# FNet mixing and a gated FFN on one core: batch 1 joins the folded sequence transform, and its tables are made a batch earlier

## The chip, the cores and the metric

The kernel runs on one core of a Trainium2 chip. The metric is the device time in microseconds (us). The engines are TensorE (PE for its matmuls, PEld for its weight loads), VectorE (DVE), ScalarE (ACT), GpSimd (POOL) and SyncE (SP, which here issues nearly all DMA transfers). Matrix products accumulate in PSUM; everything else lies in SBUF or in device memory.

## What is computed

```python
batch, seq, dim = (8, 3008, 256)
n_tokens, d_model, d_ff = (24064, 256, 1536)
...
X = np.fft.fft(x, axis=1)
X = np.fft.fft(X, axis=2)
mixed = X.real.astype(np.float32).reshape(B * S, D)
...
gate = 1.0 / (1.0 + np.exp(-(mixed @ w_gate)))
val = mixed @ w_val
return (gate * val @ w_out).astype(np.float32)
```

All is float32. The real part of a two-dimensional Fourier transform over the sequence (3008) and the features (256), and on it a gated feed-forward layer with 1536 hidden features.

## The kernel before

**The feature transform is folded into the weights.** The weights are multiplied on chip by the feature cosines and sines, which gives G1 and G2 (tables of 256 x 1536 for gate and value). What is left for each batch is the sequence transform: a cosine part pk and a sine part qk, each 128 features x 1505 frequencies. By symmetry a frequency and its mirror image come out of the same two products: their sum and their difference.

**The main loop** (L1213) has 576 iterations i: 8 batches, 6 chunks of 252 frequencies (chunk 5 has 246), 12 tiles of 128 hidden features. 72 iterations are one batch (`per`), 12 one chunk (`i0`). In iteration i:

- PE does front_a(i), the four matmuls pf<-pk; back, ten products po of an iteration five earlier with the output weights; and front_b(i), the four matmuls pf<-qk, which end what front_a began.
- ACT does the sigmoid of iteration i-1 (L880, h<-pf), the copy ae (L866) of front_a's result, the seeds of iteration i+1's PSUM (L851, pf<-ek,ge) and the second sigmoid (L894, pf<-z).
- DVE does z (L881, ae less pf), the two products h (L893, L897), and between the two one operation more (`gap[i]` where there is one, else one of the output sums c<-c of `later`). After front_b come two or three more of `later`: the output of a finished chunk as sums, 32x32 transposes (L995, os<-c) and stores (L1011, L1015).
- POOL does the sums sf<-h (L903) by which the back products need fewer matmuls.

Each engine works through its own instructions in the order of the program. Everything else is hung into this loop by tables written out by hand: `at(i, f)` puts f at the end of iteration i (any engine), `gap[i]` puts a DVE operation between the two products, `mid[i]` puts PE work in the middle. Side work is: loads and folds of the next batch's x, its sequence transform, tables and output.

**The sequence transform exists in three forms.** Batch 0 has no fold beyond the one of the mirror images and is done before the loop, with the tables ST[0] (cosines and sines of 128 partitions x 6 x 753). Batch 1 has the "half" form: x is copied by DMA to device memory (xr) in mirrored order (mirror_x, L179) in two copies of 768 KB and six of 256 KB, loaded (load_x, L147), folded by POOL and DVE (feat, across, swap, turn), and at i=64 the function `whole` does 96 pairs of matmuls of 63 rows, ev and od, for both blocks and both parts at one place. Batches from 2 on have the "quarter" form: quarter_x (L150 on, 23 DMAs: 3 that write zeros, 18 of 128 KB, 2 of 384 KB), more folding on POOL and DVE, and `quarter(b, blk)` at two places of the loop, 96 matmuls of 32 rows and 95 columns each (sum<-st), whose results are spread by DVE (quarter_ends, 19 operations placed one in each iteration).

**The tables of the quarter form are made on chip, in batch 1.** The sines and cosines come from the same input table `stab`: table_rows (L274, six DMAs to rtab in device memory, rows reversed), then quarter_load (L308, 16 DMAs into the raw tables odd and ev) and quarter_small (24 small DMAs for the factors self, other and angle), then sums on POOL and DVE (`four`, `eight`), ACT copies (`ends`, `compact`, scaling by a half) and small DVE operations (`turns`, `ratios`, `cross`: tangents and ratios). They lie at i=65 to 99 (per+1 to per+27), in a tile `st` that takes the place of batch 1's tables.

**Batch 0's first chunk** (chunk 0, whole_) has no sf sums: its output weights are WO and its product is two 504-column matmuls (po<-h,wc) in each iteration. Its two output halves are stored in 32 DMAs.

**The DMA queue.** SP issues transfers in program order; stores, loads of x, copies to xr and rtab, table loads and the rows ek for the seeds (L839) stand in one line.

Two places that a sentence can't say well: which side work stands where (`mid` and `gap` are looked up in the loop as below), and the SP-ordered copies.

```python
between = gap.pop(i, [])
if not between and later and i < count - 8:
    between = [later.pop(0)]
    n -= 1
...
mid.get(i, lambda: None)()
...
for f in side.pop(i, []):
    f()
```

Of the kernel before, what the change touches and what calls it, by code (L numbers as in the profile page):

```python
# [53 lines left out]
NQ = 6  # L54
NP = 128
# [26 lines left out]
def kernel(  # L82
# [28 lines left out]
    NJ = NO // 2 + 1  # L111
# [67 lines left out]
    def mirror_x(b):  # L179

        if b > 1:
            return quarter_x(b)

        copy = nc.sync.dma_start
        src = xf[b]
        dst = XR[b] = dram.tile([P, 4, NQ, D], F32, name=f"xr{b}")
        ops = [lambda: copy(out=dst[HP - 2 : HP, :, NQ - 1],
                            in_=zero[:, :, 0:D].to_broadcast([2, 4, D]))]

        def rows(par):  # L190
            copy(out=dst[par * HP : (par + 1) * HP, :, 0:N3], in_=src[0:HP, :, par:NQ:2])

        def mirror(par, q):
            t = M // 2 - 2 * q - par
            lo, p0, n = par * HP, t // NQ, HP - 2 * ((par, q) == (0, N3 - 1))
            copy(out=dst[lo : lo + n, :, N3 + q].rearrange("p h d -> h p d"),
                 in_=src[p0 - n + 1 : p0 + 1, :, t % NQ].rearrange("p h d -> h p d")[:, ::-1])
        for par in range(2):
            ops.append(lambda par=par: rows(par))
            ops += [lambda par=par, q=q: mirror(par, q) for q in range(N3)]  # L200
        return ops


    dt = const.tile([P, 2, D], F32, name="dt")
    ST = [const.tile([P, 2, NQ, NE + NO], F32, name="st", tag="st")]
# [14 lines left out]
    def load_table(t, q, n, lo=0, hi=NE + NO):  # L220
        nc.sync.dma_start(out=ST[0][0:NP, t, q : q + n, lo:hi], in_=stab[:, t, q : q + n, lo:hi])

    def table_again():

        full = const.tile([P, 2 * NQ * (NE + NO)], F32, name="st", tag="st")
        sizes = (2 * N3 * (NE + NO), 2 * N3 * NJ, 2 * NO, N3, N3)
        at_ = [sum(sizes[0:i]) for i in range(6)]
        st, jt, eo, *tans = [full[:, at_[i] : at_[i + 1]] for i in range(5)]
        ST[:] = [st.rearrange("p (t q k) -> p t q k", t=2, q=N3),
                 jt.rearrange("p (t q k) -> p t q k", t=2, q=N3),  # L230
                 eo.rearrange("p (h k) -> p h k", h=2), *tans]
        for t in range(2):
            for par in range(2):
                nc.sync.dma_start(out=ST[0][par * HP : (par + 1) * HP, t], in_=stab[0:HP, t, par:NQ:2])

    def table_odd():

        odd, j4 = ST[0][:, :, :, NE:], ST[1]
        pool = nc.gpsimd

        def inner(t):
            pool.tensor_tensor(j4[:, t, :, 1 : NJ - 1], odd[:, t, :, 2::2], odd[:, t, :, 1 : NO - 1 : 2],
                               op=ALU.add)

        def half(t):
            nc.scalar.mul(j4[:, t, :, 1 : NJ - 1], j4[:, t, :, 1 : NJ - 1], 0.5)

        def ends():
            pool.tensor_copy(j4[:, 0, :, 0:1], odd[:, 0, :, 0:1])
            pool.memset(j4[:, 1, :, 0:1], 0.0)  # L250

            for par in range(2):
                rows = slice(par * HP, (par + 1) * HP)
                pool.tensor_copy(j4[rows, par, :, NJ - 1 :], odd[rows, par, :, NO - 1 :])
                pool.memset(j4[rows, 1 - par, :, NJ - 1 :], 0.0)

        def tangent():
            nc.vector.reciprocal(ST[4], odd[:, 0, :, 0])
            nc.vector.tensor_tensor(ST[3], odd[:, 1, :, 0], ST[4], op=ALU.mult)
            nc.vector.tensor_scalar(out=ST[4], in0=ST[3], scalar1=-1.0, scalar2=None, op0=ALU.mult)  # L260
        return tangent, lambda: inner(0), lambda: half(0), lambda: inner(1), lambda: half(1), ends


# [14 lines left out]
    def quarter_tables():  # L278

        full = const.tile([P, 2 * NQ * (NE + NO)], F32, name="st", tag="st")  # L280
        wide = 2 * NQ4
        sizes = dict(e4=2 * N3 * NQ4, j4=2 * N3 * NQ4, r4=2 * N3 * NQ4, eo=6 * NO, tan=N3, less=N3, angle=2 * N3,
                     self=2 * N3, other=2 * N3, cx=N3, cy=N3, sign=1, odd=2 * N3 * NO, ev=2 * N3 * NE)
        lo = 0
        for name, n in sizes.items():
            TAB[name] = full[:, lo : lo + n]
            lo += n
        assert lo <= full.shape[1]
        TAB["at"] = lo - sizes["odd"] - sizes["ev"]
        TAB["full"] = full  # L290
        TAB["sums"] = full[:, TAB["at"] : TAB["at"] + 16 * wide].rearrange("p (b w x h k) -> p b w x h k", b=2, w=2, x=2,
                                                                           h=2)
        for name in ("ev", "e4", "j4", "r4", "odd"):
            TAB[name] = TAB[name].rearrange("p (t q k) -> p t q k", t=2, q=N3)
        eo = TAB["eo"].rearrange("p (i k) -> p i k", i=6)
        TAB["eo"] = [[eo[:, 4 + w].rearrange("p (h k) -> p h k", h=2) for w in range(2)],
                     [eo[:, 2 * w : 2 * w + 2] for w in range(2)]]

# [12 lines left out]
    def quarter_small(i):  # L311
        for g, par, lo in TILES:
            if i == 2:
                for t in range(2):
                    nc.sync.dma_start(out=TAB["angle"][lo : lo + TB, t * N3 : (t + 1) * N3],
                                      in_=quarter_src(g, par, t, NE))
            else:
                for h, col in enumerate((0, NE)):
                    nc.sync.dma_start(out=TAB[("self", "other")[i]][lo : lo + TB, h * N3 : (h + 1) * N3],
                                      in_=quarter_src(g ^ i, par, 0, col))  # L320

    def quarter_ops():
# [6 lines left out]
        def clear():  # L329
            for x in (j4, r4, e4):  # L330
                pool.memset(x[:, :, :, 0 :: last], 0.0)
            for g, par, lo in TILES:
                pool.memset(sign[lo : lo + TB], (1.0, -1.0)[g])

        def turns():
            vec.reciprocal(TAB["less"], TAB["angle"][:, 0:N3])
            vec.tensor_tensor(TAB["tan"], TAB["angle"][:, N3:], TAB["less"], op=ALU.mult)
            vec.tensor_scalar(out=TAB["less"], in0=TAB["tan"], scalar1=-1.0, scalar2=None, op0=ALU.mult)

        def ratios():  # L340
            vec.reciprocal(TAB["self"], TAB["self"])
            vec.tensor_tensor(TAB["other"], TAB["other"], TAB["self"], op=ALU.mult)
            vec.tensor_scalar(out=TAB["other"], in0=TAB["other"], scalar1=sign, scalar2=None, op0=ALU.mult)

        def cross():

            vec.reciprocal(TAB["cy"], ev[:, 0, :, 1])
            vec.tensor_tensor(TAB["cx"], ev[:, 1, :, 1], TAB["cy"], op=ALU.mult)
            vec.tensor_scalar(out=TAB["cx"], in0=TAB["cx"], scalar1=sign, scalar2=None, op0=ALU.mult)
            vec.tensor_scalar(out=TAB["cy"], in0=TAB["cx"], scalar1=-1.0, scalar2=None, op0=ALU.mult)  # L350
# [24 lines left out]
        return clear, (turns, lambda: eight(0), lambda: eight(1), ratios, cross), (lambda: four(0), lambda: four(1)), (  # L375
# [167 lines left out]
    def fold_ops(b, nq):  # L543
# [25 lines left out]
        if b == 1:  # L569
# [5 lines left out]
            for q in qs:  # L575
                ops += [lambda blk=blk, q=q, e=pool if q is qs[-1] else nc.vector: across(e, blk, q) for blk in range(2)]
# [7 lines left out]
        if b:  # L584
# [8 lines left out]
            tan = lambda: (ST[3], ST[4]) if b == 1 else (TAB["tan"], TAB["less"])  # L593
# [22 lines left out]
            def turn(q, minus):  # L616

                y = [slots[:, q : q + 16 : 15], slots[:, q + N3 : q + N3 + 10 : 9]]
                if minus:
                    y.reverse()  # L620
                nc.vector.scalar_tensor_tensor(
                    out=y[0][:, :, HD:D], in0=y[1][:, :, 0:HD], scalar=tan()[minus][:, q : q + 1],
# [27 lines left out]
    def half(b, w, d, blk, sn, other=None):  # L650


        c0, n = ((0, NE), (NE, 2 * NJ if b else NO))[blk]
        ev, od = [bank(name, other and other[i])[:, 0:n] for i, name in enumerate(("ev", "od"))]

        def sums(*qs):
            for q in sorted(qs, key=lambda q: q % 2):
                mm((ev, od)[q % 2], w(q), ST[0][0:NP, int(sn), q, c0 : c0 + n], q < 2, q >= NQ - 2)

        def both():  # L660

            for r in range(2):
                for q in range(N3):
                    for par, sum_ in enumerate((ev, od)):
                        rows = slice(par * HP, par * HP + HP - 1 - (par and q == N3 - 1))
                        if blk:
                            out_, wq = sum_[:, r * NJ : (r + 1) * NJ], q + N3 * r
                            tab = ST[1][rows, r ^ int(sn), q]
                        else:
                            out_, wq = sum_[:, r::2], q + N3 * (r ^ int(sn))  # L670
                            tab = ST[0][rows, int(sn), q, r:NE:2]
# [634 lines left out]
```

## Time and profile before

| | |
|---|---|
| time, median of 3 runs | 1912.32 us (1912.19 to 1915.45) |
| the profiled execution | 1912.46 us, of which the span (first to last instruction) is 1910.7 us |
| TensorE clock granted | 1.00 |
| busy PE, DVE, ACT, POOL | 99%, 79%, 71%, 81% of the span |
| one iteration of the loop | 3.12 us (3.05 to 3.09 in chunk 5) |
| one batch, from i=144 to 216 | 230.5 us; batch 1, from 72 to 144, 233.3 us |
| DMA | 58 GB/s in the mean, 652 stores of 56 and 7 KB |

The profile gives busy times of each engine, the chain of waits that ended last, groups of instructions by source line, what each wait was for, and a timeline. An iteration of the loop is read from PE's timeline as the distance between two successive groups pf<-pk.

### The profile page before, as it was taken

Reading aid. Unit: us, or ns where it says so; the run is one execution under the profiler, and the core shown is the slowest. Engines: PE = TensorE matmul, PEld = TensorE weight load, DVE = VectorE, ACT = ScalarE, POOL = GpSimd, SP = SyncE. Lnnn points to the kernel's source line nnn. Section 1 sums busy time; section 2 is a strip of 40 time slices with the busy share of each in tenths; the row PEclk is TensorE's granted clock in tenths of the full one; section 3 lists DMA queues with packets and bytes.
Section 4 is the critical chain, followed back from the end, with each engine's and each line's share of the span. In section 5 each row is a group of like instructions: output and inputs, shape, how many; then the busy total and the mean of one; then the engine's idle time right before and its main releaser. Section 6 shows DMA issues by size and latency. Waiting matters only on the chain.

```text
span 1910.7 us, 35839 instructions
## 1 busy us (share of the span) xinstructions
PE 1899.5 (99%) x11740; PEld 1759.9 (92%) x11740; DVE 1513.2 (79%) x3351; ACT 1351.7 (71%) x3219; POOL 1543.8 (81%) x2742
## 2 busy tenths in 40 slices
PE   8999999999999999999999999999999999999999
PEld 5789999899999999999999999999999999999998
DVE  7677777878979778787788878888788787977775
ACT  4877767767777777767777777777767777777775
POOL 2489969987999779997799878999789986877770
PEclk9999999999999999999999999999999999999999
DMA  8353234312122121221211222112120220011011
GB/s 314 109 98 68 71 102 100 77 39 81 20 61 59 31 84 26 69 42 36 88 37 52 45 39 81 39 50 56 30 76 16 36 39 14 15 24 18 15 18 30
DMA packets 198833, 110.05 MB, mean 58 GB/s; under 512 B 139269, under 2 KB 189168, under 8 KB 196856
## 3 DMA queue, kind: packets, MB, share of 16 engines
q1 hardware_dynamic: 198070, 107.25, 23.5%
q8 instruction: 94, 1.54, 0.3%
q14 instruction: 91, 0.75, 0.1%
q10 hardware_dynamic: 546, 0.51, 0.1%
q0 software_dynamic: 32, 0.00, 0.0%
HBM read 73.56 MB, written 47.87 MB: 64 GB/s over the span
## 4 chain that ended last, share of the span: by engine, by line
PE 97%; DMA 1%; DVE 1%; ACT 1%; POOL 1%; issue 0%; SPq 0%; ACTq 0%; DVEq 0%; POOLq 0%
PE pf L134 51%; PE po L134 43%; PE sum L134 2%; DMA x<-in_xf_dram 1%; PE ps L134 1%; PE ev L134 1%; DMA raw<-in_moe_w_val_dram 0%; PE od L134 0%; POOL sf L903 0%; DVE z L881 0%; POOL x L563 0%; ACT ae L866 0%; PE pe L134 0%; DVE wf L451 0%; ACT wl L533 0%
## 5 line engine op out<-in xcount | busy, mean ns | idle before, releaser
L903 POOL TENSOR_TENSOR sf<-h,sf 128x168 f32<-128x168 f32 (+1 forms) x1104 | 617.7, 579 | 74.2 <-DVE h L897 71.9
L903 POOL TENSOR_TENSOR sf<-h 128x168 f32<-128x168 f32 (+1 forms) x920 | 520.7, 585 | 167.9 <-DVE h L897 165.7
L134 PE MATMUL pf<-qk,G 128*128 128x252 f32 (+1 forms) x2304 | 583.5, 376 | 0.9 <-ACT ae L866 0.8
L134 PE MATMUL pf<-pk,G 128*128 128x252 f32 (+1 forms) x2304 | 582.9, 376 | 0.3 <-ACT pf L851 0.3
L851 ACT ACTIVATE pf<-ek,ge 128x252 f32<-128x252 f32 (+1 forms) x1142 | 538.3, 471 | 20.9 <-DVE h L897 1.1
L134 PE MATMUL po<-sf,wf 128*128 128x168 f32 (+1 forms) x2944 | 508.3, 305 | 0.0
L866 ACT ACTIVATE ae<-pf 128x504 f32<-128x504 f32 (+1 forms) x576 | 338.9, 588 | 219.4 <-PE pf L134 218.4
L134 PEld LDWEIGHTS pf<-pk,G 128*128 128x128 f32 x2304 | 436.0, 190 | 53.8 <-ACT pf L851 1.7
L897 DVE TENSOR_TENSOR h<-pf,z 128x252 f32<-128x252 f32 (+1 forms) x576 | 240.7, 418 | 283.7 <-ACT pf L894 280.8
L134 PE MATMUL po<-h,wf 128*128 128x168 f32 (+2 forms) x2584 | 461.0, 307 | 0.0
L134 PEld LDWEIGHTS po<-sf,wf 128*128 128x128 f32 x2944 | 453.4, 190 | 8.0
L881 DVE TENSOR_TENSOR z<-ae,pf 128x504 f32<-128x504 f32 (+1 forms) x576 | 384.9, 668 | 81.8 <-ACT h L880 77.6
L987 DVE TENSOR_TENSOR c<-c 128x168 f32<-128x168 f32 (+1 forms) x920 | 443.1, 504 | 3.2
L134 PEld LDWEIGHTS pf<-qk,G 128*128 128x128 f32 x2304 | 410.5, 190 | 32.7 <-ACT ae L866 2.3
L134 PEld LDWEIGHTS po<-h,wf 128*128 128x128 f32 x2584 | 410.5, 190 | 17.6 <-issue 0.9
L880 ACT ACTIVATE h<-pf 128x252 f32<-128x252 f32 (+1 forms) x576 | 217.0, 377 | 152.5 <-PE pf L134 133.8
L894 ACT ACTIVATE pf<-z 128x252 f32<-128x252 f32 (+1 forms) x576 | 214.0, 372 | 110.5 <-DVE h L893 107.9
L893 DVE TENSOR_TENSOR h<-h,pf 128x252 f32<-128x252 f32 (+1 forms) x576 | 233.2, 405 | 0.0
L903 POOL TENSOR_TENSOR sf<-sf 128x168 f32<-128x168 f32 (+1 forms) x184 | 101.4, 551 | 14.4
L903 POOL TENSOR_TENSOR sf<-sf,h 128x168 f32<-128x168 f32 (+1 forms) x184 | 109.7, 596 | 0.0
L970 ACT COPY c<-po 128x504 f32<-128x504 f32 (+1 forms) x138 | 78.5, 569 | 0.0
L995 DVE STREAM_TRANSPOSE os<-c 128x256 f32<-128x256 f32 x188 | 77.1, 428 | 0.5 <-issue 0.3
(166 smaller groups left out, 888.1 us busy)
## 6 DMA issues: line engine op xcount, KB each, us to landing
x<-xr SPq DMA_DIRECT2D x14, 1536.0 KB
out_dram<-os SPq DMA_DIRECT2D x368, 56.0 KB
xr<-in_xf_dram SPq DMA_DIRECT2D x90, 128.0 KB
x<-x SPq DMA_DIRECT2D x96, 96.0 KB
ek<-ed SPq DMA_DIRECT2D x40, 126.0 KB
xr<-in_xf_dram SPq DMA_DIRECT2D x12, 384.0 KB
out_dram<-os SPq DMA_DIRECT2D x284, 7.0 KB
x<-in_xf_dram SPq DMA_DIRECT2D x3, 1024.0 KB
```

Source lines behind the costliest of these rows:

```text
L134: nc.tensor.matmul(o, l, r, start=start, stop=stop, skip_group_check=True)
L851: nc.scalar.activation(PF[i][:, g], EK[i // NFT], AF.Copy, scale=ge[:, g, f : f + 1])
L866: nc.scalar.activation(AP[i], PF[i], AF.Copy, scale=2.0)
L880: nc.scalar.activation(H[p][:, fh, 0:n], PF[i][:, 0], AF.Sigmoid)
L881: nc.vector.tensor_tensor(z[:, :, ::-1], AP.pop(i), PF[i], op=ALU.subtract)
L893: nc.vector.tensor_tensor(h[:, fh, 0:n], h[:, fh, 0:n], pf[:, 1], op=ALU.mult)
L894: nc.scalar.activation(pf[:, 0], z[:, 0], AF.Sigmoid)
L897: nc.vector.tensor_tensor(h[:, fh, n:], pf[:, 0], z[:, 1], op=ALU.mult)
L903: nc.gpsimd.tensor_tensor(block(p, dst), block(p, a), block(p, b), op=(ALU.subtract, ALU.add)[op])
L970: (nc.vector.tensor_copy if t == 1 or t == 3 else nc.scalar.copy)(C[0][:, 3 * t * R : 3 * (t + 1) * R], PO[t][:, 0 : 3 * R])
L987: nc.vector.tensor_tensor(t[:, dst * R : (dst + 1) * R], *v, op=(ALU.subtract, ALU.add)[op])
L995: nc.vector.transpose(os_[0][:, s, 0:nb, h, :], t[:, c0 : c0 + nb * TB])
```

## The change

- Batch 1 takes the quarter form too: quarter_x(1) (23 DMAs at i=9 to 14) in place of mirror_x(1), load_x(1) one iteration later (i=14), `quarter(1, blk)` at mid[53] and mid[65] in place of `whole` at i=64, its swaps, turns and end operations in gaps of i=35 to 76. `half`'s second form, table_again and table_odd fall away.
- The tables of the quarter form are made in batch 0. The tile ST is split in two, st0 (cosines) and st1 (sines). When batch 0 is transformed, the raw tables (odd, ev) are loaded into the place of st1: table_rows at i=15 and 16, quarter_load at 21 and 22. The made tables go to st0 at i=42; the operations that make them lie at i=43 to 52.
- The small factors (self, angle) are copied from the raw tables by eight ACT copies, four each at the end of i=30 and 31, into a tile `small`; `other` comes from `self` by four DMAs inside SBUF (i=32). The DVE operations on them lie in gaps of i=31 to 44. The 24 small DMAs are gone.
- e_load(b), the loads for the e rows, moves from i=14+b to 22+b. One of the six `across` operations moves from POOL to DVE; the fold of batch 2 has other places; load_x(2) moves from i=65 to 66.
- Batch 0's chunk 0: the output weights are read with a stride of two columns, so that one 32x32 transpose holds every second feature and two of them make 64 adjacent ones; its stores are 16 instead of 32.

In all, PE has 5920 instructions instead of 5872, DVE 3370 instead of 3353, ACT 3240 instead of 3224, POOL 2738 instead of 2747, SP 1178 instead of 1188.

```diff
-    ST = [const.tile([P, 2, NQ, NE + NO], F32, name="st", tag="st")]
+    ST = [const.tile([P, NQ, NE + NO], F32, name=f"st{t}", tag=f"st{t}") for t in range(2)]
...
+    def raw_tables():
+        full = TAB["full"] = place(1, dict(odd=2 * N3 * NO, ev=2 * N3 * NE))
+        TAB["sums"] = full[:, 0 : 32 * NQ4].rearrange("p (b w x h k) -> p b w x h k", b=2, w=2, x=2, h=2)
+
+    def made_tables():
+        n = 2 * N3 * NQ4
+        place(0, dict(e4=n, j4=n, r4=n, eo=6 * NO))
...
-    def quarter_small(i):
+    def quarter_small(which):
+
         for g, par, lo in TILES:
-            if i == 2:
-                for t in range(2):
-                    nc.sync.dma_start(out=TAB["angle"][lo : lo + TB, t * N3 : (t + 1) * N3],
-                                      in_=quarter_src(g, par, t, NE))
-            else:
-                for h, col in enumerate((0, NE)):
-                    nc.sync.dma_start(out=TAB[("self", "other")[i]][lo : lo + TB, h * N3 : (h + 1) * N3],
-                                      in_=quarter_src(g ^ i, par, 0, col))
+            at_ = slice(lo, lo + TB)
+            if g == which:
+                nc.scalar.copy(TAB["self"][at_, 0:N3], TAB["ev"][at_, g, :, 0])
+                nc.scalar.copy(TAB["angle"][at_].rearrange("p (t q) -> p t q", t=2),
+                               TAB["odd"][at_, :, :, 0] if g == 0 else TAB["odd"][at_, ::-1, :, 0])
+
+    def quarter_other():
+        for g, par, lo in TILES:
+            o = lo + (TB, -TB)[g]
+            nc.sync.dma_start(out=TAB["other"][lo : lo + TB], in_=TAB["self"][o : o + TB])
...
-            w = WO[f // 2][:, f % 2]
+            w = WO[f // 2].rearrange("p f (m h) -> p f h m", h=2)[:, f % 2]
             for h in range(2):
-                mm(PO[h][:, 0 : 2 * n], w[:, h * P : (h + 1) * P], H[p][:, part], f == 0, f == NFT - 1)
+                mm(PO[h][:, 0 : 2 * n], w[:, h], H[p][:, part], f == 0, f == NFT - 1)
...
-    for i, f in enumerate(mirror_x(1)):
-        at(i0 - 3 + i // 2, f)
-    at(i0 + 1, lambda: load_x(1))
+    for i, f in enumerate(quarter_x(1)):
+        at(i0 - 3 + i // 4, f)
+    at(i0 + 2, lambda: load_x(1))
     for b in range(1, B):
-        at(i0 + 2 + b, lambda b=b: e_load(b))
+        at(22 + b, lambda b=b: e_load(b))
...
+    for i in range(NQ):
+        at(15 + i // 3, lambda i=i: table_rows(i % 2, i // 2))
+    at(20, raw_tables)
+    for i in range(4):
+        at(21 + i // 2, lambda i=i: quarter_load(i // 2, i % 2))
+    signs, ratios = small_ops()
+    at(i0, signs)
+    for i in range(2):
+        at(30 + i, lambda i=i: quarter_small(i))
+    at(32, quarter_other)
+    for i, f in zip((33, 33, 34, 41, 42, 42, 31, 32, 44, 44), ratios, strict=True):
+        gap.setdefault(i, []).append(f)
...
         for i, f in enumerate(TURN.pop(1)):
-            at(58 + i, f)
+            gap[35 + i] = [f]
+        swaps, last, first = MORE.pop(1)
+        at(41, swaps[1])
+        at(52, swaps[0])
...
-    for blk in (1, 0):
-        at(g0, *[lambda blk=blk, what=what: whole(1, blk, what)() for what in range(2)])
-    at(g0 + 1, lambda: load_x(2))
...
-    for i in range(NQ):
-        at(g0 + 1 + i, lambda i=i: table_rows(i % 2, i // 2))
-    at(per + 1, quarter_tables)
-    for i in range(4):
-        at(per + 2 + i, lambda i=i: quarter_load(i // 2, i % 2))
-
-    for i in range(3):
-        at(per + 6 + i, lambda i=i: quarter_small((2, 0, 1)[i]))
...
+    for blk in range(2):
+        mid[(5 - blk) * i0 + 5] = lambda blk=blk: quarter(1, blk)
+    at(54, first_ends)
+    at(per - 6, lambda: load_x(2))
```

## The prediction

> **What bounds the kernel now.** I read the page first: busy time and the chain of waits.
>
> ```profile
> PE 1899.5 (99%) x11740; PEld 1759.9 (92%) x11740; DVE 1513.2 (79%) x3351; ACT 1351.7 (71%) x3219; POOL 1543.8 (81%) x2742
> ...
> PE 97%; DMA 1%; DVE 1%; ACT 1%; POOL 1%; issue 0%; SPq 0%; ACTq 0%; DVEq 0%; POOLq 0%
> ```
>
> TensorE (PE) sets the time: 99% busy, 97% of the chain. So an edit pays only where PE does less or stands less, and costs only where PE is made to wait; the other engines count through that alone. PE's waits after the first 100 us come to 1.1 us. A wait of PE understates a stall, however, since its weights may load and its matmuls stretch meanwhile; I therefore also took the starts of successive pf<-pk groups in PE's timeline, one for each iteration i of the main loop. They lie 3.12 us apart (3.05 to 3.09 in chunk 5), except: i=64, 11.46; i=90 to 97, 3.74 4.16 3.69 3.23 3.25 3.15 3.16 3.23; i=107 and 108, 3.22 and 3.15; and two of 6.19 in each batch from 2 on. Each is a place that the change touches. PE's timeline shows i=64 and one of the 6.19:
>
> ```profile
> 255.47 0.99 PE L134 MATMUL pf<-qk,G 128*128 128x246 f32 x4
> 256.39 0.42 PE L134 MATMUL ev<-st,x 63*128 63x189 f32 x1
> ...
> 264.67 1.10 PE L134 MATMUL pf<-pk,G 128*128 128x246 f32 x4
> ...
> 415.97 1.01 PE L134 MATMUL pf<-qk,G 128*128 128x252 f32 x4
> 417.76 2.93 PE L134 MATMUL sum<-st,x 32*128 32x95 f32 x96
> ```
>
> The half transform of batch 1 holds PE from 256.39 to 264.67; a quarter transform takes 2.93 us for 96 small matmuls.
>
> **What goes.** (1) Batch 1's transform: i=64 costs 11.46-3.09 = 8.37 us more than its neighbours; two quarters cost 2 x (6.19-3.12) = 6.14. Gain 2.23 us. (2) The stalls of i=90 to 97, 107 and 108 add up to 2.78 us over 3.12 each. There DVE, ACT and POOL make the tables (st<-st) while they do batch 2's folds. The tables move to batch 0, the folds stay; I take 2.5 us of the 2.78 as gain (between 2.0, if some contention with the folds stays, and 2.78).
>
> **What is added on the DMA queue.** SP issues in program order, so each transfer that is moved counts. Its waits and its timeline around the raw tables:
>
> ```profile
> SPq L1015 <- DMA rtab<-in_stab_dram: 3.6, 1, 3.6
> ```
>
> ```profile
> 264.81 0.81 SPq L147 DMA_DIRECT2D x<-xr  x2
> 265.67 17.16 SPq L274 DMA_DIRECT2D rtab<-in_stab_dram  x6
> ...
> 294.14 0.32 SPq L1011 DMA_DIRECT2D out_dram<-os  x1
> 298.07 0.34 SPq L1015 DMA_DIRECT2D out_dram<-os  x1
> ```
>
> The store at 298.07 shares no data with a copy to rtab and yet waited 3.6 us for the last of them: the eighth transfer before it. So a transfer here waits for the one eight places earlier to land. The stretches show the rates (columns: PE, PEld, DVE, ACT, POOL, granted clock, DMA share, GB/s):
>
> ```profile
> 223.00:227.00 4.00, 4.00 (x26) 3.82 (x25) 3.36 (x9) 2.81 (x7) 3.92 (x8) 1.00 0.29 100
> 227.00:231.00 4.00, 4.00 (x25) 3.80 (x25) 3.31 (x8) 2.95 (x8) 3.84 (x9) 1.00 0.26 91
> 266.00:274.00 8.00, 8.00 (x50) 7.65 (x49) 5.98 (x16) 5.67 (x14) 5.49 (x11) 1.00 0.91 378
> 274.00:286.00 12.00, 12.00 (x73) 11.46 (x72) 8.83 (x23) 8.34 (x20) 9.76 (x16) 1.00 0.13 51
> ```
>
> Row by row: the folded copies to xr (1 and 2) use about a quarter of the 16 engines, 95.5 GB/s; the load of x all of them; the copies to rtab an eighth, 51 GB/s. These start only when x has drained (264.81 to 274.2: 9.4 us) and the six last until 298.0, 4.0 us each.
>
> In the changed order this is what comes:
> - Batch 1's copies to xr become 18 folded ones of 128 KB (2.36 MB at 95.5 GB/s: 24.7 us) and two of 384 KB (0.79 MB at 378 GB/s: 2.1 us). Before, they began at 80.8 and the load of x was issued at 104.79. Now 80.8+24.7+2.1, and some 2 us for landing and issue: x at 110, drained at 119.5 (9.4 us later).
> - Three copies to rtab follow; they land at 123.5, 127.5 and 131.5. Behind them stand eight stores of chunk 0, and the eighth waits for the third copy. Only then are copies 4 to 6 issued; they land at 137, 141 and 145.
> - Then the next eight stores wait for these, and the 16 loads of the raw tables (quarter_load) start at about 146. The same 16 went at 0.58 to 0.63 us each after 303.5, so the thirteenth lands at 146+13 x 0.6+about 1.2 = 155, the last at 157.
>
> **Who waits for it.** The small factors become eight ACT copies, four after i=30 and four after i=31; the last of the first four reads what the thirteenth load brings. ACT's timeline:
>
> ```profile
> 147.16 0.36 ACT L894 ACTIVATE pf<-z 128x252 f32<-128x252 f32 x1
> 148.09 0.38 ACT L880 ACTIVATE h<-pf 128x252 f32<-128x252 f32 x1 [0.57 <-PE pf L134]
> ```
>
> ACT comes to the copies at 147.5 and stands until 155. Queued behind are h (148.09), ae and the seeds of the next iteration, without which PE cannot go on. In the unstalled rows h ends 0.6 us after the iteration's start; in the stalled ones of i=90 to 97 PE was late only where it ended more than about 1.65 after. i=31 starts at 147.8. So h ends at 155+0.19 (a small ACT copy)+0.38 = 155.6, against 149.45 allowed: PE loses **6.1 us**. The range: 0.9 if x is issued at 104.8 as before (5.2 us sooner), 9 if the loads land 3 us later (the longest wait of a store, 3.6, once more); no row shows this wait itself.
>
> PE then starts again after some 6 us of idling. The nearest row is the start of the kernel:
>
> ```profile
> 5.73 3.78 PE L134 MATMUL warm<-dt 128*128 128x256 f32 x8 [5.73 <-DMA dt<-in_dtab_dram]
> 9.31 2.83 PE L134 MATMUL ps<-raw,dt 128*128 128x256 f32 x8
> ...
> 41.51 1.89 PE L134 MATMUL ps<-wqk,dt 128*128 128x256 f32 x8
> ```
>
> Eight such matmuls take 1.89 us warm, 3.78 and 2.83 in the first two groups: (3.78-1.89)+(2.83-1.89) = 2.8 us lost. Whether an idle time in mid-kernel costs that, no row shows: 0 to 2.8, I take the middle, 1.4. The Trainium skill (TensorE: Matmul & The Clock Gate, "Part 1: The HAM clock gate (the "warmup" mystery)") says that the clock falls to half after one idle window of about 3.4 us and needs about as long a busy stretch to come back; the start rows agree with the second half, no row yet shows the first. By it an estimate is 1.7 us lost, and the sum would be 0.3 higher.
>
> **DVE, ACT and POOL in batch 0.** By the rows' means (z 0.668, the two products 0.405 and 0.418, c sums 0.504, transposes 0.43, an x operation 0.76 to 0.84, a table sum 1.10, small ones 0.17 to 0.54) DVE's work of i=42 to 49 in the new order adds up to 30.5 us, against 8 x 3.12 = 25.0: 5.5 too much. In before, i=87 to 95 come to 7.2 too much in the same way and stalled 2.64; so some 4.6 are taken up by slack (DVE may run behind with the c sums), and 5.5 leaves 0.9. ACT has 3.4 to 3.6 us of work in each of i=50 to 52. I take **0.8 us** in all (0 to 2.6, the old stall). For i=65 to 72, with two of the quarter's end operations each, the same sum is 3.0 too much: below 4.6, nothing.
>
> **At nothing:** the 24 small DMAs that go (SP never held PE there), and 16 instead of 32 stores for batch 0's chunk 0 (PE waits for no store; they only shorten SP's queue). The 24 weight loads of that chunk at stride 2: a load takes 190 ns beside matmuls of 504 columns that come 0.46 us apart (po<-h,wc: 1.85 us for four), so twice the time is still covered; no row shows a strided load, and if each took 0.2 us more than its cover, 24 of them would cost 4.8. e_load 8 iterations later: its first reader is e_fold at i=36, after the 157 of above (i=36 starts at 163.5 plus the stall).
>
> **The sum**, on the profiled execution (1912.46 us, 0.14 above the median): -2.23-2.5+6.1+1.4+0.8 = +3.6, so **1916.0**. About 0.2% (3.8 us) is what a measurement of this kernel can tell from no change; this lies just inside it.
>
> **Rivals.**
> - *B, the loads land in time.* If the folded copies run beside more of the queue, or rtab beside x, ACT finds its rows at 147.5: no stall, no cold clock. -4.7+0 to 0.8: 1907.7 to 1908.5, **1908.1**, faster. For: with x issued at 104.8 the loss is only 0.9, so one us more does it. Against: 18 of the 20 copies ahead of x now run on a quarter of the engines.
> - *C, a short wait.* x is issued 4 us sooner than I reckon, ACT waits some 2 us beyond its slack and the clock stays: -4.7+2+0.8, **1910.5**, no change.
> - *D, slower: the vector engines of i=42 to 52 stall PE as well.* Price: from the old 2.64 up to all of DVE's 5.5, 4 us, beside A's stall: -4.7+6.1+1.4+4 = +6.8, **1919.3**. It decides as soon as DVE's c sums run at their slow form (0.67) rather than the fast one (0.32), which both occur; for it, that POOL's folds now run there too; against, that DVE comes rested out of the stall of i=31.
>
> **How the numbers follow.** My case A (1912.5 to 1919.5) 0.60, half a point either side of the bound 1916.1 being about even: same 0.30, slower 0.30. B 0.16 (faster), C 0.10 (same), D 0.14 (slower). So faster 0.16, same 0.40, slower 0.44. The range reaches from B's low end, 1907.5, to D's with part of the stall's bound of 9, 1921.5.
>
> **What would show it.** A: in the changed trace ACT waits at the copies (small<-st) around 147 to 155 for a load of st, one iteration at 31 of about 9 us, PE's clock below 1.00 just after. The six rtab copies in two threes with stores between. i=64 gone, two iterations of 6.2 at 53 and 65, i=90 to 97 at 3.12. Wrong it is if x is issued before 105 and rtab lands before 136, if the stretch behind i=31 shows no slow matmuls, or if iterations outside 30 to 52 change their length, chunk 0's stride-2 weights (i=17 on) above all.

## The result and the profile after

The changed kernel takes **1921.05 us** (median of 6 runs, 1920.04 to 1921.97) against 1912.5 for the kernel before beside it: a ratio of 1.0042 (95% interval 1.0029 to 1.0055), 0.4% slower. The forecast was 1916.0, in a range of 1907.5 to 1921.5. The profiled execution's span is 1919.2 us, 8.5 more than before.

The page's lines for busy time and for the chain, after:

```profile
PE 1899.2 (99%) x11836; PEld 1758.9 (92%) x11836; DVE 1518.2 (79%) x3368; ACT 1354.3 (71%) x3235; POOL 1544.9 (81%) x2733
...
PE 93%; DMA 3%; POOL 1%; DVE 1%; ACT 1%; SPq 0%; issue 0%; ACTq 0%; POOLq 0%
```

PE's busy time is as before (1899 us), so the longer span is time in which it stood; and 3% of the chain is now DMA, which was 1%. PE's waits after the first 100 us say where:

```profile
PE pf L133 <- ACT ae L781: 8.6, 3, 8.2
PE po L133 <- POOL sf L818: 0.8, 2, 0.4
```

One wait of 8.2 us, for ACT. ACT's timeline and PE's at that place:

```profile
149.91 0.39 ACT L809 ACTIVATE pf<-z 128x252 f32<-128x252 f32 x1 [0.81 <-DVE h L808]
152.43 0.19 ACT L255 COPY small<-st 32x3 f32<-32x3 f32 x1 [2.14 <-DMA st<-in_stab_dram]
156.48 0.20 ACT L256 COPY small<-st 32x6 f32<-32x6 f32 x1 [3.85 <-DMA st<-in_stab_dram]
...
159.20 0.20 ACT L256 COPY small<-st 32x6 f32<-32x6 f32 x1 [2.31 <-DMA st<-in_stab_dram]
159.42 0.38 ACT L795 ACTIVATE h<-pf 128x252 f32<-128x252 f32 x1
```

```profile
150.50 1.59 PE L133 MATMUL po<-sf,wf 128*128 128x168 f32 x10
160.34 2.05 PE L133 MATMUL pf<-qk,G 128*128 128x252 f32 x4 [8.25 <-ACT ae L781]
162.18 1.89 PE L133 MATMUL pf<-pk,G 128*128 128x252 f32 x4
```

ACT came to the first copy at 150.3 and left the fourth at 159.4; the sigmoid h stood behind them. PE's groups then take 2.05 and 1.89 us, where they take 1.01. The stretches (PE, PEld, DVE, ACT, POOL, granted clock, DMA share, GB/s) show the clock at half:

```profile
160.00:162.00 2.00, 1.66 (x4) 1.42 (x5) 0.97 (x4) 1.90 (x7) 0.40 (x1) 0.50 1.56 12
162.00:164.00 2.00, 2.00 (x6) 1.59 (x6) 2.00 (x7) 0.61 (x3) 1.33 (x2) 0.50 0.93 6
164.00:166.00 2.00, 2.00 (x15) 1.93 (x14) 0.42 (x3) 1.84 (x4) 0.00 (x0) 1.00 0.85 19
```

What each stretch of the loop costs more than in the kernel before, from the starts of the pf<-pk groups (us; minus is a gain; e2 and e3 ran once each):

| kernel | time | before beside it | i=0-11 | 27-30 | 31-37 | 45-52 | 86-109 |
|---|---|---|---|---|---|---|---|
| after | 1921.05 | 1912.5 | 0.0 | 1.8 | **10.3** | 0.65 | -1.95 |
| e1_copies33 | 1924.09 | 1912.35 | 0.0 | 0.5 | 14.4 | 0.7 | -2.1 |
| e2_copies31 | 1918.02 | 1912.35 | 0.0 | 0.8 | 8.4 | 0.7 | -2.1 |
| e3_copies32 | 1915.23 | 1912.35 | 0.0 | 2.1 | 4.4 | 0.7 | -2.0 |
| e5_x_early | 1915.31 | 1912.35 | 3.1 | 0.0 | 2.2 | 0.7 | -0.7 |
| e4_rows_early | 1918.39 | 1912.93 | 6.8 | 1.4 | 0.1 | 1.6 | -1.9 |
| e6_rows_early_fwd | 1918.18 | 1912.93 | 8.6 | 0.0 | 0.0 | 1.4 | -1.8 |
| e7_before_stores | 1913.37 | 1912.93 | 0.0 | 0.0 | 0.0 | 0.0 | 0.0 |
| e8_folds2 | 1918.56 | 1912.93 | 7.0 | 0.0 | 0.0 | 1.4 | 0.1 |
| e9_split | 1913.4 | 1914.32 | 0.0 | 0.0 | 4.7 | 0.7 | -1.9 |
| e10_split_folds | 1913.12 | 1914.32 | 0.0 | 0.0 | 6.0 | 0.7 | -2.4 |
| e11_thirds | 1909.41 | 1912.2 | 0.0 | 0.0 | 0.0 | 1.4 | -2.5 |
| e12_small_early | 1908.93 | 1912.32 | 0.0 | 0.0 | 0.0 | 1.0 | -2.5 |

Batch 1's transform is worth the same in every kernel that has it in the quarter form: 3.06 more at i=53, 5.42 less at i=64 and 65, together -2.36. For after: 1.82+10.31+0.65-1.95-2.36 = 8.5, the whole difference of the spans. (The kernel before takes some 1912.5 us in most executions and about 3 us more in others, hence the 1914.32 beside e9 and e10. The columns come from one profiled execution each: e5's column 86-109 holds 1.3 us at i=101 to 104, e8's 0.8, and the others nothing there.)

### The profile page after: what moved, and what is told of

Same layout as the page of the kernel before. It is cut to its first block, busy times and chain, and to the rows that moved or that the text cites. A ratio compares the mean times of both kernels' runs of the same rounds, so it can differ in the third digit from the quotient of the medians.

```text
span 1919.2 us, 36048 instructions
## 1 busy us (share of the span) xinstructions
PE 1899.2 (99%) x11836; PEld 1758.9 (92%) x11836; DVE 1518.2 (79%) x3368; ACT 1354.3 (71%) x3235; POOL 1544.9 (81%) x2733
## 4 chain that ended last, share of the span: by engine, by line
PE 93%; DMA 3%; POOL 1%; DVE 1%; ACT 1%; SPq 0%; issue 0%; ACTq 0%; POOLq 0%
PE pf L133 49%; PE po L133 41%; PE sum L133 2%; DMA rtab<-in_stab_dram 2%; DMA x<-in_xf_dram 1%; POOL sf L818 1%; PE ps L133 1%; DMA raw<-in_moe_w_val_dram 0%; DMA st<-in_stab_dram 0%; SPq L247 0%; PE ev L133 0%; PE od L133 0%; POOL x L505 0%; DVE z L796 0%; DVE c L902 0%
## 5 line engine op out<-in xcount | busy, mean ns | idle before, releaser
L818 POOL TENSOR_TENSOR sf<-sf 128x168 f32<-128x168 f32 (+1 forms) x184 | 101.1, 549 | 14.4
```

Source lines behind the costliest of these rows:

```text
L818: nc.gpsimd.tensor_tensor(block(p, dst), block(p, a), block(p, b), op=(ALU.subtract, ALU.add)[op])
```

## The experiments

Theory W: ACT's copies of the small factors wait for the raw tables, which stand at the end of a chain on SP's queue (folded copies of x, load of x, copies to rtab with stores between, raw tables). Rival Q: the queue is late for everybody; whoever reads next waits instead, and moving ACT's copies gains little.

**e1_copies33: ACT's copies three iterations later.**

```diff
-        at(30 + i, lambda i=i: quarter_small(i))
-    at(32, quarter_other)
+        at(33, lambda i=i: quarter_small(i))
+    at(34, quarter_other)
-(33, 33, 34, 41, 42, 42, 31, 32, 44, 44)
+(34, 34, 35, 35, 42, 42, 35, 44, 44, 44)
```

(and the turns in gaps 36 to 41, the swap at 42)

> The changed kernel with all eight ACT copies of the small factors at the end of i=33 (turns one iteration later, reciprocals at 34 and 35), nothing else. Theory W (ACT stands at the copies until the thirteenth raw-table load lands at 159.2, PE behind it): ACT comes to i=33's copies at about 159.7, so i=31 and 32 last 3.1 us instead of 12.53 and 4.03, and the time falls by 10.3 us to about 1910.7. Rival Q (the late queue only moves the wait: turns, ratios or the made tables stand for the same transfers next): the time falls by less than 5 us, to 1916 or more, with new stalls at i=34 to 45.

Measured: 1924.09 us (ratio 1.0062, 1.0045 to 1.0079), slower still. i=31 and 32 last 3.12, as W said; then i=34 to 37 lose 14.4 us. ACT's waits between 160 and 180:

```profile
ACT pf L766 <- DVE h L812: 7.4, 1, 7.4
ACT pf L766 <- DMA ek<-ed: 4.7, 1, 4.7
```

The row ek that seeds i=36 stands behind the 16 table loads and three of the loads of the e rows, and landed 4.7 us late. The 7.4 us are of my making: I put the reciprocal of `self` into gap 35, where it has to wait until the four DMAs of `other`, further back on the same queue, have read `self`; DVE stood for 13.1 us, and h with it. So Q is right for this kernel: in after, ek is in time only because the stall at i=31 lets it catch up.

**e2_copies31 and e3_copies32: one and two iterations later.**

```diff
 e2:
+        at(31 + i, lambda i=i: quarter_small(i))
+    at(33, quarter_other)
 e3:
+        at(32, lambda i=i: quarter_small(i))
+    at(33, quarter_other)
 both:
+(33, 33, 34, 41, 42, 42, 44, 44, 44, 44)
```

> The changed kernel with the ACT copies one iteration later (i=31 and 32, tangent ratios of DVE to 44). Theory W: the load still lands at 159.2, i=32 starts 3.1 us later than i=31 did, so the wait costs 5.3 us instead of 8.4. If an idle time over about 3.4 us costs the clock, another 1.9 us at a granted clock of 0.5 for about 4 us: 7.2 in all, time about 1918. If the clock's loss grows with the idle time, about 1.2 instead.

> The changed kernel with all ACT copies at i=32. Theory W: the wait costs 2.2 us (8.4 less two iterations). If only an idle time over about 3.4 us costs the clock, the granted clock stays at 1.0 and the time is about 1912.9; if any stall costs in proportion, 0.5 us more.

Measured, one run each: 1918.02 us, a loss of 8.4 at i=32 and 33; and 1915.23, a loss of 4.4 at i=33 and 34. Each iteration of delay takes some 3 us from the wait (e2 also came to its copies 1.0 us sooner, since it lost less at i=27 to 30). The clock is the surprise. In e3 PE waited 2.5 us at most, and yet:

```profile
159.00:161.00 2.00, 0.14 (x1) 0.14 (x2) 0.65 (x2) 1.84 (x8) 1.92 (x5) 1.00 1.62 62
161.00:163.00 2.00, 2.00 (x6) 1.65 (x7) 1.74 (x6) 1.46 (x4) 2.00 (x5) 0.57 0.79 6
163.00:165.00 2.00, 2.00 (x8) 1.75 (x8) 1.97 (x5) 0.77 (x2) 2.00 (x4) 0.57 0.82 6
```

Of the 4.4 us lost the wait itself is 2.5; the other 1.9 are the clock, for some 4 us after the idle time. My condition "over about 3.4 us" was wrong: a shorter wait is enough here.

**e5_x_early: batch 1's copies and load of x three iterations earlier.**

```diff
-        at(i0 - 3 + i // 4, f)
-    at(i0 + 2, lambda: load_x(1))
+        at(i0 - 6 + i // 4, f)
+    at(i0 - 1, lambda: load_x(1))
```

> The changed kernel with batch 1's folded copies to xr and its load of x three iterations earlier (i=6 on, load at 11). Theory W with its chain (folded copies, x, rtab, stores, raw tables, ACT): every link comes some 7 to 10 us sooner, the thirteenth load lands at about 150 and i=31 loses 1 us or less; and if the 1.84 us at i=27 to 29 come from x landing late for POOL's folds, they go too: about 1909.5. If those come from the closer places of the folds, they stay: about 1911.4. Rival: the copies only take longer beside the weight loads, x no earlier than 111: no gain, 1920.

Measured: 1915.31 us (ratio 1.0014, 1.0004 to 1.0023). x is issued at 104.1 instead of 111.4; i=27 to 30 lose nothing, so those 1.8 us came from x; i=31 loses 2.2. But i=0 to 11 lose 3.1, since the start's weights share the queue with the copies: ACT waits 4.7 us for the biases ge, in after 1.1. PE's wait at i=31 is 1.8 us, and the clock stays:

```profile
153.00:155.00 2.00, 0.23 (x2) 0.00 (x0) 0.49 (x1) 1.08 (x4) 2.00 (x6) 1.00 1.55 110
155.00:157.00 2.00, 1.99 (x9) 1.57 (x10) 1.02 (x5) 1.89 (x8) 1.92 (x4) 1.00 0.79 4
```

It stays at 1.00, too, after a longer wait in the same run: 2.7 us at i=9 (80.4 to 83.0), for the seeds that stood behind ge.

**e4_rows_early: the copies to rtab at i=3 to 8; e6_rows_early_fwd: also the forward copies of x over more engines.**

```diff
 e4 and e6:
-        at(15 + i // 3, lambda i=i: table_rows(i % 2, i // 2))
+        at(3 + i, lambda i=i: table_rows(i % 2, i // 2))
 e6, in run():
+            if step > 0 and b == 1:
+                copy(out=dst[lo + skip : lo + skip + n, :, q], in_=rows[:, :, t % NQ])
+                return
```

> The changed kernel with the six copies to rtab at i=3 to 8 (before batch 1's folded copies) instead of i=15 and 16. Theory W: with the six copies of 4 us and the store that waits for the third out of the chain, the raw-table loads follow the load of x and the stores, at about 124 instead of 148.5; the thirteenth lands at about 135, ACT does not wait, the e rows and ek come sooner too, and i=31 and 32 last 3.1: 10.3 us less, 1910.7. The 1.84 us at i=27 to 29 stay if they come from x, which is issued at 111 as before. Rival: the six copies hold the weight loads of the start up, and what is gained at i=31 is lost at i=3 to 11 (up to 4 us for each copy that a weight load stands behind).

> As e4_rows_early, and the 6 of 18 folded copies of batch 1 that run forwards are written with the 32 rows ahead of the 4 streams, so that they spread over all engines. If those copies are slow because only 4 rows stand ahead (1.37 us each at 95.5 GB/s), they take 0.35 each, x is issued some 6 us sooner, at about 105, and the 1.84 us at i=27 to 29 go as well: 1908.9. If x stays at 111, the number of rows ahead is not what sets the rate, and the time is that of e4.

Measured: 1918.39 (ratio 1.0030, 1.0019 to 1.0040) and 1918.18 (1.0023, 1.0013 to 1.0033). W's part holds: without the copies to rtab in the chain, i=31 to 37 lose 0.1 and 0.0 us. The rival's part holds too: i=0 to 11 lose 6.8 and 8.6. ACT's waits in e4 between 60 and 95 name the biases that a load brings back from device memory, 1.1 us for the same in after:

```profile
ACT pf L766 <- DMA ge<-G: 8.7, 4, 4.8
```

In e6 the load of x goes out 28.5 us after the first large copy to xr (86.5 to 115.1), in e4 32.2 (86.8 to 119.0): 3.7 us sooner, not 6, and enough for i=27 to 30. The Trainium skill (DMA: Bandwidth & Descriptors, "Why a DMA increments its semaphore by 16 and not by 1") says that the slowest dimension of both sides, as the instruction carries it, sets how many of the engines a transfer uses, the largest number up to 16 that divides it. The runs agree where the first dimension is 2 or 4 (shares of 0.13 and 0.26 to 0.29). Two of the six forward copies have 31 rows of 4 pieces, which e6's trace records as 124 pieces in one dimension; the other four are recorded as 128. By that rule the two use 4 engines, no more than before, and the four use 16. e6's stretches agree: the second copy of 31 rows (issued at 93.1) passes without a rise of the share, which is 0.27 from 92 to 99, while it rises at copies of 32 rows, such as the last (issued at 107.6; 0.62 from 109.5 to 110.5). The first of 31 rows runs beside a large copy, where the share can't tell. So four copies gain where six were reckoned: an estimate of 4 x (1.37-0.35) = 4.1 us, against 3.7 measured.

e6's start also shows that the length of a wait alone does not settle the clock. PE's two waits there, and the stretch after each:

```profile
75.80 1.12 PE L133 MATMUL pf<-pk,G 128*128 128x252 f32 x4 [3.61 <-ACT pf L769]
87.32 1.66 PE L133 MATMUL pf<-pk,G 128*128 128x252 f32 x4 [2.43 <-ACT pf L769]
```

```profile
76.00:77.00 1.00, 1.00 (x5) 0.86 (x5) 0.42 (x1) 1.00 (x3) 0.00 (x0) 1.00 0.12 48
88.00:89.00 1.00, 1.00 (x4) 0.83 (x3) 0.02 (x1) 0.98 (x3) 0.00 (x0) 0.50 0.95 306
```

After 3.6 us of idling the clock stayed, after 2.4 it fell.

**e7_before_stores: the kernel before with the stores' part alone** (strided weights, transposes into strided places, 16 stores; the same lines as in the change).

> The kernel before with one part of the change alone: chunk 0's weights at stride 2 and its stores in 16 transfers. All theories: no change, 1912.4 within 0.5, and iterations 5 to 16 as long as before (5.12 and 3.39); a strided weight load that is not covered would show there as up to 4.8 us.

Measured: 1913.37 us, ratio 1.0005 (0.9996 to 1.0014). All iterations from 0 to 71 last as in the kernel before: the strided weight loads cost nothing, and half the stores bring nothing.

**e8_folds2: e6 with batch 2's folds where the kernel before had them.**

```diff
-            slots = [s0 + i for i in (-2, -1, -1, 0, 0, 1, 2, 2, 4, 6, 8, 9, 11, 12, 13, 15, 17)]
+            slots = [s0 + i for i in (-3, -2, -1, -1, 0, 1, 2, 2, 11, 12, 12, 13, 14, 14, 15, 16, 17)]
```

> As e6_rows_early_fwd, and batch 2's folds on POOL at the iterations where the kernel before had them (11 to 17 instead of 4 to 17 after the batch's start). The changed kernel still loses 0.8 us at i=91 to 96, where DVE's turns wait for POOL's folds just before them. If the places of the folds cause it, this number changes by more than 0.3 us against e6; if it is the turns' own load on DVE, it stays at 0.8. Time within 1 us of e6.

Measured: 1918.56 us. i=90 alone now loses 1.7, i=86 to 98 come to -0.6 instead of e6's -1.7. The places of POOL's folds do set what is lost there.

**e9_split and e10_split_folds: the queue in another order.** The eight loads of g=0, which need no reversed rows, go ahead of the copies to rtab; ACT's copies for g=1 come two iterations after those for g=0.

```diff
+    at(20, raw_tables)
+    for i in range(4):
+        at(20, lambda i=i: quarter_load(i // 2, i % 2, 0))
+    for i in range(NQ):
+        at(20 + i // 3, lambda i=i: table_rows(i % 2, i // 2))
+    for i in range(4):
+        at(22, lambda i=i: quarter_load(i // 2, i % 2, 1))
...
+        at(30 + 2 * i, lambda i=i: quarter_small(i))
+    at(33, quarter_other)
 e10 only:
+            slots = [s0 + i for i in (-3, -2, -2, -1, -1, 0, 0, 1, 2, 4, 6, 8, 9, 11, 12, 13, 15)]
```

(with e6's forward copies, e3's gaps, and rtab at 20 and 21)

> The changed kernel with the queue put in another order and nothing left out: the eight raw-table loads that need no reversed rows (g=0) at i=20, behind the stores, then the six copies to rtab (i=20 and 21), then the other eight loads (i=22); ACT copies g=0's factors at i=30 and g=1's at i=32 (DMA for the other at 33, four small DVE operations at 44); the six forward folded copies of batch 1 spread over all engines as in e6. Theory W (each reader waits for what stands ahead of its load): g=0's loads land before 135, g=1's at about 155, both ahead of ACT; x is issued near 107.5 and POOL is not late: i=27 to 36 all 3.1. What is left against the kernel before is -2.24 (two quarters for one half transform), -1.97 (i=90 to 108) and +0.7 (i=46 to 52): 1908.9. Rival: ek or the e rows, 14 us of small pieces ahead of them on the same queue, come too late and PE stops at i=36 as in e1, 1912 or more.

> As e9_split, and batch 2's folds on POOL one place earlier each (3 before the batch's start to 15 after, instead of 2 before to 17 after). If i=91 to 96 lose 0.8 us because DVE's turns wait for POOL, the 0.8 falls below 0.4, and the time is 0.4 to 0.8 below e9; if the turns' own DVE time does it, nothing changes.

Measured: 1913.4 (ratio 0.9994, 0.9986 to 1.0003) and 1913.12 (0.9992, 0.9983 to 1.0001), level with the kernel before. g=0's copies no longer wait and i=27 to 32 are clean, but g=1's loads only start at 148.6, when the last copy to rtab has landed; ACT waits there 2.8 us at one go, and with the clock 4.7 and 6.0 us are lost at i=33 and 34 (the clock was at half for 3.4 us in e9 and for 6.8 in e10). In e10 i=86 to 109 come to -2.4 instead of -1.9: the 0.5 us was DVE's turns waiting for POOL. Since e10, however, 0.2 us is lost at i=78, which e9 does not lose.

**e11_thirds: each copy to rtab in two, with three column groups ahead.**

```diff
-        nc.sync.dma_start(
-            out=rtab[par * TB : (par + 1) * TB, :, q].rearrange("p t k -> t p k"),
-            in_=stab[p0 - TB + 1 : p0 + 1, :, qq].rearrange("p t k -> t p k")[:, ::-1])
+        for t in range(2):
+            nc.sync.dma_start(
+                out=rtab[par * TB : (par + 1) * TB, t, q].rearrange("p (c k) -> c p k", c=3),
+                in_=stab[p0 - TB + 1 : p0 + 1, t, qq].rearrange("p (c k) -> c p k", c=3)[:, ::-1])
```

> As e10_split_folds, and each of the six copies to rtab is issued as two (cosines, sines) with its rows cut in three column groups ahead, 96 pieces of 1 KB in place of 32 of 3 KB. In e9 and e10 these copies (4.0 us each, the last lands at 148.5) still keep g=1's loads until 159 and cost a stall of 4.7 to 6.0 us at i=33 and 34. If the number of rows ahead sets how many DMA engines a copy uses (2 before, 3 now), all six take 16 instead of 24 us, g=1's loads land at about 151, before ACT's copies at 156, and the stall goes: 1912.9-6.0+1.8 = 1908.7, faster than the kernel before by 0.2%. Rival: they run no faster or ek, behind the e rows, is late for i=36: 1912 or more.

Measured: **1909.41 us** (1909.22 to 1909.79), ratio 0.9984 (0.9975 to 0.9993). SP's queue, e10 first:

```profile
125.89 11.20 SPq L209 DMA_DIRECT2D rtab<-in_stab_dram  x6
148.41 6.59 SPq L250 DMA_DIRECT2D st<-rtab  x8
```

```profile
125.53 14.05 SPq L210 DMA_DIRECT2D rtab<-in_stab_dram  x12
142.42 5.83 SPq L251 DMA_DIRECT2D st<-rtab  x8
```

The same bytes are through 6 us sooner, and the stall is gone. That closes the case for W: against e10 nothing was left out, only the queue is faster.

**e12_small_early: four small DVE operations out of gap 44.**

```diff
-(33, 33, 34, 41, 42, 42, 44, 44, 44, 44)
+(33, 33, 34, 41, 42, 42, 33, 34, 34, 34)
```

> As e11_thirds, and the four small DVE operations for cx and cy, which e11 has in gap 44, at 33 and 34. e11 still loses 1.4 us at i=45 to 52, the changed kernel 0.65 there (with two of the four in gap 44, two at 31 and 32). If DVE's sum of work in these iterations sets it, as the prediction reckoned, taking 0.38+0.24+0.10+0.05 us from gap 44 brings i=45 to 52 to 0.3 to 0.7 and the time to about 1908.6. Rival: the loss comes from the wait for the swap's DMAs or from POOL; then it stays at 1.4 and the time at 1909.4.

Measured: **1908.93 us** (1908.62 to 1909.39), ratio 0.9980 (0.9971 to 0.9989), faster than both kernels. i=45 to 52 lose 1.0 instead of 1.4. In e11 the chain of waits ran through DVE there, without a gap, from 188 to 199; now i=45 to 47 and 49 to 52 are clean, and one loss of 0.9 at i=48 is left, where the chain runs through POOL:

```profile
196.34 2.83 POOL sf L822 x5
...
199.73 4.00 POOL sf L822 x7
...
203.79 0.73 POOL sf L822
204.53 0.68 POOL st L299
...
205.22 0.68 ACT st L322
```

So DVE's load was one cause and POOL's is the next; how much of the changed kernel's own 0.65 each had is open.

## Why the prediction was right

The sign and the mechanism of the likeliest case held; 1921.05 lies at the upper end of the range, 5 us above the point and 0.45 below the bound. Of these 5 us, 2.3 are the wait of ACT, 1.8 a step that the sum did not have, and about 0.5 each the clock and the tables. That the range held the sum of them owes something to luck: its top was set by other terms. By its steps, predicted and measured:

| step | predicted | measured |
|---|---|---|
| half transform for two quarters | -2.23 | -2.36 |
| tables leave batch 1 | -2.5 (-2.0 to -2.78) | -1.95; -2.5 with the folds earlier (e10, e11) |
| ACT waits for the thirteenth load | +6.1 (0.9 to 9) | +8.4 |
| clock after it | +1.4 (0 to 2.8) | +1.9 |
| DVE and ACT at i=42 to 52 | +0.8 (0 to 2.6) | +0.65 |
| i=27 to 30 | nothing | +1.8 |
| stores, strided weights | 0 | 0 (e7) |

- **The chain** ran link by link as worked out, each link a little late: x issued at 111.4 (110 predicted), the third copy to rtab landed at 133.2 (131.5), the sixth at 148.1 (145), the thirteenth load at 159.2 (155). The wait of a store for the transfer eight places ahead came twice, as the order said:

```profile
SPq L925 <- DMA rtab<-in_stab_dram: 7.2, 2, 3.6
```

- **The step that was mis-sized** is therefore this sum: 1.4 us at x, 1.7 more through the two groups of three copies, and 1.1 at the loads, whose landing (0.8 us each from the first issue at 148.5) and not their issue (0.47) set the pace. The load was 4.2 us later than reckoned and i=31 itself started 1.85 later (149.65): 6.1+4.2-1.85 = 8.45. 10.3 us were lost at i=31 and 32; the wait is 8.4 if the clock is counted as 1.9 (two groups of four matmuls 1.04 and 0.88 longer than 1.01).
- **The step that was missing:** that x, 6.6 us later than before, has a reader of its own. POOL's folds of batch 1 stand at i=20, and POOL waited there 2.5 us:

```profile
POOL x L496 <- DMA x<-xr: 2.5, 1, 2.5
```

  After it POOL was without a gap, sf late, and PE lost 1.8 us at i=27 to 30. I priced x only as a link to the tables. e5, e6 and e9 to e12, with x some 4 to 10 us sooner by the loop's own progress, lose nothing there. The prediction had named a change of length outside i=30 to 52 as a sign of being wrong, and here it came (i=27 and 29), though not at the strided weights where it was looked for.
- **The clock.** The rule of the Trainium skill (TensorE: Matmul & The Clock Gate, "Part 1: The HAM clock gate (the "warmup" mystery)") gave 1.7, nearer to the 1.9 than my middle. Its other half, that an idle window of about 3.4 us is needed, the runs do not bear out as a length of the wait: waits of 2.4 (e6), 2.5 (e3) and 2.6 us (e9) halved the clock, waits of 1.8 and 2.7 (e5) and 3.6 (e6) did not. The traces agree with the 3.4 us as the length of a window, but not all of it has to be idle. By the clock that the traces record, it stays at half in mid-kernel for 3.41 us (e3, e4, e6, e8, e9) or for twice that (after, e2, e10), and the fall at a kernel's end comes a whole number of such steps after the one in the middle (516 in after, 514 in e10). So the clock is set in steps of 3.41 us that run on through the kernel, wherever a wait begins. It fell after each step that held 2.05 us (e10) or more of idling, and after none that held 1.92 or less: e6's wait of 3.6 us was cut by a step's end into 1.92 and 1.70, e5's of 2.7 into 1.6 and 1.1 (its steps counted back from the fall at its end). The bound between 1.92 and 2.05 is read from these runs; no run was made to test it.
- **Rival D** had the right time (1919.3) for the wrong reason: DVE's sum of work cost 0.65, not 4. The 0.8 for this step came near by luck: counted in the changed trace in the way that gives 7.2 for the old stall, DVE has 3.9 us too much at i=42 to 49 (5.5 reckoned) and 4.8 at i=65 to 72 (3.0 reckoned), so against a slack of 4.6 the first should have lost nothing and the second a little. The first lost 0.65 and the second nothing; e12 shows POOL beside DVE as a cause.
- **Rival B** (the loads land in time) describes e11: it needs a faster queue, and then the change is worth 0.15 to 0.2%.

## What to carry to other kernels

When work is moved earlier, follow the transfer queue to the reader: add up each link (rate of the slowest copy, the wait for a transfer some places ahead, the landing) and compare it with the time at which the first reader comes by; then do so for every other reader of every link, since moving one reader only finds the next (e1). A transfer whose outermost dimension is small runs at a fraction of the rate, and rewriting it (e11) removed the stall that new places in the queue had only shortened or moved. A wait of a few us in the engine that sets the time can cost more than its length: some 2 us of slow clock, once 3.3, came on top of most waits of 2.4 us or more, but not of all.

## What the runs showed of the hardware

- The granted clock fell to 0.50 for 3.41 or 6.83 us, in steps that do not start with the wait. It fell after steps with 2.05 to 3.41 us of idling of PE, not after steps with 1.92 us or less; so waits of 2.4 to 2.8 us (e6, e3, e9, e10) lowered it, and waits of 2.7 (e5) and 3.6 us (e6) did not. The loss on top of the wait was 1.9 to 2.1 us (e3, e2, e9, after) and 3.3 in e10.
- Small-piece loads are slow on the queue: seven loads of the e rows and one ek between them hold SP for 15 us (155.3 to 170.5 in e9), and ek, one transfer of 126 KB behind three of them, landed about 5 us after its issue (e1: issued at 162.9, ACT went on at 168.1).
- Copies with a first dimension of 2 moved 51 GB/s, with 4 some 95, with 16 or more 350 to 378; cutting a copy's columns into three groups ahead brought the time from the first copy's issue to the loads behind the last from 22.5 to 16.9 us.
